# The last FFN step on its own PSUM tiles, its output in halves, and 128-column scores in tile 0

## The chip, the cores and the metric

One core of one Trainium2 chip runs the whole program. The metric is the device time of one execution in microseconds; a smaller number is better. Three executions were timed without the profiler, and one more was profiled.

## The reference

Attention with a window of 96 keys and 8 global keys feeds a feed-forward layer with a rational activation. Everything is fp32; the shapes are batch 4, 8 heads, 768 positions, 64 per head, so 3072 tokens of 512, and 2048 hidden units.

```python
scores = scale * q @ k.T + bias              # kept where key < n_global, or 0 <= rel < n_local
a = softmax(scores)
x = (a @ v).transpose(0, 2, 1, 3).reshape(3072, 512)
h = x @ w_in                                 # 512 x 2048
P = a0 + a1*h + a2*h**2 + a3*h**3
Q = 1 + |b0|*|h| + |b1|*h**2
out = (P / (Q + 1e-6)) @ w_out               # 2048 x 512
```

## The kernel before

The tokens are cut into 24 tiles of 128 queries, six to a batch; two tiles make a chunk of 256 tokens, and there are 12 chunks. Attention goes in 96 units, one for a tile and a pair of heads. A query tile sees its own block of 128 keys and the block before it. Tile 0 of a batch has no block before it: its score product (`st_score`, L407) reads the one block twice by a broadcast, so that it is 256 columns wide like the others, and the softmax reads the first 128 columns alone. That concerns 16 units (4 in each batch), with 4 score products each.

The FFN goes in 96 steps, eight to a chunk, each for 256 hidden units in two halves `y` of 128. A step runs `st_ffn1` (the first product into a PSUM tile `h`, 12 products of 256 columns for each half, since x and w are each split into a high and a low part), `st_ew1` to `st_ew4` (the activation, on ScalarE, VectorE and GpSimd, with `q` in PSUM and `g` in SBUF as its ends) and `st_ffn2` (12 products of 512 columns into the accumulators `acc_0` and `acc_1`, one for each half of the tokens). For chunk 0 the weights are not split yet, and the products are plain fp32 (L249, L328).

The loop over `t` writes the stages down with priorities (the tables `PRI`, `PRI_A`), and a scheduler orders the instructions of each engine when the program is built. During the first 35 steps or so the weights are loaded, decoded and split between the other work (`decode`, `split_w`), for the most part on VectorE.

The last step, 95, is written apart: `is_last(f)` puts its activation through `last_half`, once for each half, with VectorE in GpSimd's place. Both halves lie in one PSUM tile `h95`, and the loop asks for the second half's product behind the first half's activation:

```python
            if is_last(f):
                st_ew4(f - 1)
                last_half(f, 0)
                st_ffn1(f, 1)
                last_half(f, 1)
```

After it the two accumulators are copied out (one on ScalarE, one on VectorE) and SyncE's queue sends each as 128 rows of 2 KB (`st_ffn2`, L339 and L342). Then each engine reads a flag and branches past the general version of the kernel (L671, L672), which these inputs don't need.

Of the kernel before, what the change touches and what calls it, by code (L numbers as in the profile page):

```python
# [9 lines left out]
F32 = mybir.dt.float32  # L10
# [3 lines left out]
AF = mybir.ActivationFunctionType  # L14
# [80 lines left out]
def tile_kernel(ctx: ExitStack, tc: tile.TileContext, q, k, v, n_global, n_local,  # L95
# [144 lines left out]

    def st_ffn1(f, y):
        c, j = divmod(f, FPC)
        if y == 0:
            hps[f] = pl.ps_h.tile(sh, F32, tag="h", name=f"h{f}")
        jw, fw = divmod((2 * j + y) * P, 2 * TOK)
        fs = slice(fw, fw + P)
        if c == 0 and not pl.split:
            for ct in range(NCT):
                nc.tensor.matmul(out=hps[f][:, y, :], lhsT=full[1, ct, jw][:, fs], rhs=xT[c][:, ct, :],  # L249
                                 start=(ct == 0), stop=(ct == NCT - 1))  # L250
            return
        xh, xl = xT[c]
        n = 0
        for ct in range(NCT):
            wh, wl = w_hi((1, ct, jw)), low[1, ct, jw]
            for w, x in ((wh, xh), (wh, xl), (wl, xh)):
                nc.tensor.matmul(out=hps[f][:, y, :], lhsT=w[:, fs], rhs=x[:, ct, :],  # L257
                                 start=(n == 0), stop=(n == 3 * NCT - 1))
                n += 1

# [4 lines left out]
    def is_last(f):  # L265
        return f == NU - 1 and not pl.split
# [4 lines left out]


    def st_ew1(f, ys=BOTH):
        h = hps[f][:, ys]
        if f not in ew:
            ew[f] = {}
        for n in "uas":
            if n not in ew[f]:
                ew[f][n] = tmp(f"f{n}{f}")
        u, a, s = (ew[f][n][:, ys] for n in "uas")  # L280
        nc.scalar.activation(out=u, in_=h, func=AF.Identity, scale=a3, bias=a2)  # L281
        nc.scalar.activation(out=a, in_=h, func=AF.Abs, scale=b0)
        nc.scalar.activation(out=s, in_=h, func=AF.Square, scale=b1)  # L283

    def st_ew2(f, ys=BOTH):
        h = hps[f][:, ys]
        u, a, s = (ew[f][n][:, ys] for n in "uas")
        nc.vector.tensor_tensor(out=u, in0=u, in1=h, op=ALU.mult)  # L288
        nc.vector.scalar_tensor_tensor(out=u, in0=u, scalar=a1, in1=h, op0=ALU.add, op1=ALU.mult)  # L289
        side(f).tensor_tensor(out=a, in0=a, in1=s, op=ALU.add)  # L290


    def st_ew3(f, ys=BOTH):
        if f not in rps:
            rps[f] = pl.ps_r.tile(sh, F32, tag="r", name=f"q{f}")
        a, s = (ew[f][n][:, ys] for n in "as")
        nc.scalar.activation(out=s, in_=a, func=AF.Ln, bias=q1)  # L297
        nc.scalar.activation(out=rps[f][:, ys], in_=s, func=AF.Exp, scale=-1.0)  # L298

    def st_ew4(f, ys=BOTH):  # L300
        u, a, r = ew[f]["u"][:, ys], ew[f]["a"][:, ys], rps[f][:, ys]
        nc.vector.scalar_tensor_tensor(out=u, in0=u, scalar=a0, in1=r, op0=ALU.add, op1=ALU.mult)  # L302
        nc.vector.scalar_tensor_tensor(out=r, in0=a, scalar=q1, in1=r, op0=ALU.add, op1=ALU.mult)  # L303
        nc.vector.scalar_tensor_tensor(out=u, in0=r, scalar=2.0, in1=u, op0=ALU.subtract, op1=ALU.mult,  # L304
                                       reverse0=True)
        if f < FPC and not pl.split:
            gs[f] = u
            return
        if f not in gs:
            gs[f] = pl.ffn.tile([P, 2, 2, TOK], FR, tag="g", name=f"g{f}", bufs=pl.gbufs)  # L310
        g = gs[f]
        nc.scalar.copy(out=g[:, 0, ys], in_=u)  # L312
        side(f).tensor_tensor(out=g[:, 1, ys], in0=u, in1=g[:, 0, ys], op=ALU.subtract)  # L313
# [2 lines left out]
        for st in (st_ew1, st_ew2, st_ew3, st_ew4):  # L316
            st(f, slice(y, y + 1))

    def st_ffn2(f, t):
        c, j = divmod(f, FPC)  # L320
        if j == 0:
            accs[c, t] = pl.ps_o.tile([P, DM], F32, tag="acc", name=f"acc{c}_{t}")
        acc = accs[c, t]
        ts = slice(t * P, (t + 1) * P)
        for y in range(2):
            ft = 2 * j + y
            if c == 0 and not pl.split:
                nc.tensor.matmul(out=acc, lhsT=gs[f][:, y, ts], rhs=full[0, ft],  # L328
                                 start=(ft == 0), stop=(ft == NFT - 1))
                continue  # L330
            wh = w_hi((0, ft))
            for n, (z, w) in enumerate(((0, wh), (0, low[0, ft]), (1, wh))):
                nc.tensor.matmul(out=acc, lhsT=gs[f][:, z, y, ts], rhs=w,  # L333
                                 start=(ft == 0 and n == 0), stop=(ft == NFT - 1 and n == 2))
        if j == FPC - 1:
            o = tmp(f"o{c}_{t}").rearrange("p a b -> p (a b)")
            rows = slice(c * TOK + t * P, c * TOK + (t + 1) * P)
            if is_last(f):
                (nc.vector.tensor_copy if t else nc.scalar.copy)(out=o, in_=acc)  # L339
            else:  # L340
                nc.any.tensor_copy(out=o, in_=acc)
            nc.sync.dma_start(out=out[rows, :], in_=o)  # L342


# [54 lines left out]
    def st_score(u):  # L399
        c, t, p, b, i = unit(u)  # L400
        qT = qTs.pop(u)
        s_ps = pl.ps_t.tile([P, 2, 2, P], F32, tag="t", name=f"s{u}")
        for x in range(2):
            h = 2 * p + x
            rhs = kT[:, h] if i else kT[:, h, 0:1, :].broadcast_to([P, 2, P])
            for z in range(2):
                nc.tensor.matmul(out=s_ps[:, x], lhsT=qT[:, z, x, :], rhs=rhs, start=(z == 0), stop=(z == 1))  # L407
        if 1 <= i < NT - 1:
            nc.gpsimd.tensor_copy(out=kT[:, 2 * p:2 * p + 2, i % 2, 0:G], in_=kG[:, 2 * p:2 * p + 2, :])
        if i == 0:  # L410
            mk = mask0
        else:
            mk = masks[:, 0:2, :] if i % 2 else masks[:, 1:3, :]
        pr = pl.att.tile([P, 2, 2, P], F32, tag="prob", name=f"pr{u}")
        st = stats[:, u % 4]
        for x in range(2):
            h = 2 * p + x
            nc.vector.tensor_tensor_reduce(  # L418
                out=blocks_of(pr[:, x], i), in0=blocks_of(s_ps[:, x], i), in1=mk,
                scale=-(2.0 ** -(h + 1)), scalar=3e38, op0=ALU.add, op1=ALU.min, accum_out=st[:, x:x + 1])  # L420
        prob[u] = (pr, st)
# [71 lines left out]
    def windowed():  # L493
# [17 lines left out]
        for t in range(NU + LAG + F2):  # L511
# [10 lines left out]
            on("score", st_score, t - 2)  # L522
            on("soft", st_soft, t - 2)
            on("ffn1a", st_ffn1, f, 0)
            on("qkT", st_qkT, t)
            if t % 2:
                on("pv", lambda u: st_pv(u // 2), t - 5)
# [8 lines left out]
            if is_last(f):  # L536
                st_ew4(f - 1)
                last_half(f, 0)
                st_ffn1(f, 1)
                last_half(f, 1)  # L540
            else:
                on("ffn1b", st_ffn1, f, 1)
                on("ew1", st_ew1, f)
                if not is_last(f - 1):
                    on("ew4", st_ew4, f - 1)
                on("ew2", st_ew2, f)
            on("ffn2a", st_ffn2, f - F2, 0)
            on("pT", st_pT, t - 3)
            on("ffn2b", st_ffn2, f - F2, 1)
# [161 lines left out]
```

## Time and profile before

| | |
|---|---|
| median of the three timed executions | 796.09 us (795.2 to 796.21) |
| the profiled execution's own time | 793.47 us |
| its span, first to last instruction | 791.7 us |
| TensorE busy, share of the span | 745.0 us, 94% |
| VectorE busy, share of the span | 589.6 us, 74% |
| mean granted clock of TensorE | 0.996 of full speed |

The span is what the trace covers; 1.8 us of the execution's own time lie outside it. A share over the whole span mixes three stages: the start with the weights, the long middle, and the last microseconds.

### The profile page before, as it was taken

To read this page: it belongs to the slowest core of one execution; us is meant where nothing else is said; L and a number is where in the kernel's file an instruction comes from. 1 tells how busy PE (TensorE), PEld (TensorE's weight loads), DVE (VectorE), ACT (ScalarE), POOL (GpSimd) and SP (SyncE) were. 2 spreads that over 40 slices of the span, in tenths; PEclk is the share of its full clock that TensorE was granted. 3 is DMA by queue.
4 is the path that set the end of the run, shared out by engine and by line. 5 is a ranking of instruction groups with operands and counts; after the bars stand their busy time and mean duration, and the time that the engine had idled before them with its cause. 6 is when DMAs were issued, how large, how long until landed. Compare 5 with 4: busy or idle time off the path is not lost.

```text
span 791.7 us, 15480 instructions
## 1 busy us (share of the span) xinstructions
PE 745.0 (94%) x5184; PEld 647.2 (82%) x5184; DVE 589.6 (74%) x1453; ACT 573.0 (72%) x1407; POOL 531.7 (67%) x572
## 2 busy tenths in 40 slices
PE   3678998899999999999999999999999999999995
PEld 2466656598988998988998988988998988988993
DVE  5899998988786767776776767776776767776664
ACT  4688767776786777777777777777777777776763
POOL 3887657998966676675676676675677676664440
PEclk9999999999999999999999999999999999999999
DMA  7884555122121222222222222222222222100000
GB/s 182 233 228 144 158 156 159 44 65 64 43 58 23 62 55 49 62 54 58 57 47 49 61 55 48 61 55 53 63 48 48 61 56 48 41 15 1 27 1 32
DMA packets 101400, 55.90 MB, mean 71 GB/s; under 512 B 81856, under 2 KB 94144, under 8 KB 101312
## 3 DMA queue, kind: packets, MB, share of 16 engines
q1 hardware_dynamic: 101312, 54.82, 26.3%
q8 instruction: 44, 0.72, 0.4%
q14 instruction: 44, 0.36, 0.1%
HBM read 35.92 MB, written 6.29 MB: 53 GB/s over the span
## 4 chain that ended last, share of the span: by engine, by line
PE 81%; DVE 9%; POOL 3%; DMA 2%; issue 2%; ACT 1%; SPq 0%; DVEq 0%; POOLq 0%; ACTq 0%
PE h L257 32%; PE acc L333 30%; PE s L407 5%; PE o L467 5%; PE tp L450 4%; PE tk L377 3%; POOL pr L440 2%; PE acc L328 1%; DMA qT<-qT 1%; DVE pr L418 1%; DMA r<-in_moe_w_out_dram 1%; DVE fu L304 1%; POOL sp L369 1%; DVE fu L288 1%; DVE r L189 1%
## 5 line engine op out<-in xcount | busy, mean ns | idle before, releaser
L333 PE MATMUL acc<-wout_h,g 128*128 128x512 f32 x704 | 250.1, 406 | 0.8 <-ACT g L312 0.8
L257 PE MATMUL h<-xh,win_h 128*128 128x256 f32 x704 | 204.7, 291 | 2.4 <-DVE fu L289 2.4
L440 POOL TENSOR_SCALAR pr<-pr,stats 128x256 f32<-128x256 f32 (+1 forms) x192 | 180.5, 950 | 32.9 <-DVE stats L433 15.5
L257 PE MATMUL h<-xl,win_h 128*128 128x256 f32 x704 | 197.7, 281 | 0.0
L290 POOL TENSOR_TENSOR fa<-fa,fs 128x512 f32<-128x512 f32 x95 | 124.5, 1311 | 91.1 <-ACT fs L283 87.3
L333 PEld LDWEIGHTS acc<-wout_h,g 128*128 128x128 f32 x704 | 128.5, 188 | 23.3 <-ACT g L312 1.2
L257 PEld LDWEIGHTS h<-xh,win_h 128*128 128x128 f32 x704 | 132.5, 188 | 11.3 <-issue 6.6
L369 POOL TENSOR_TENSOR sp<-nat,sp 128x256 fp32r<-128x256 f32 x96 | 75.9, 791 | 95.8 <-DVE sp L368 45.8
L257 PEld LDWEIGHTS h<-xl,win_h 128*128 128x128 f32 x704 | 132.4, 188 | 1.8 <-issue 0.5
L428 ACT ACTIVATE pr<-pr,stats 128x256 f32<-128x256 f32 (+1 forms) x192 | 92.6, 485 | 55.2 <-DVE stats L418 55.0
L281 ACT ACTIVATE fu<-h,coef 128x512 f32<-128x512 f32 (+1 forms) x97 | 75.0, 774 | 60.3 <-PE h L257 59.4
L313 POOL TENSOR_TENSOR g<-fu,g 128x512 fp32r<-128x512 f32 x87 | 112.7, 1295 | 7.9 <-DVE fu L289 4.5
L302 DVE SCALAR_TENSOR_TENSOR fu<-fu,coef,q 128x512 f32<-128x512 f32 (+1 forms) x97 | 71.6, 738 | 48.2 <-ACT q L298 47.2
L297 ACT ACTIVATE fs<-fa,coef 128x512 f32<-128x512 f32 (+1 forms) x97 | 69.6, 718 | 34.9 <-POOL fa L290 32.5
L452 DVE COPY pT<-tp 128x512 f32<-128x512 f32 (+1 forms) x75 | 48.5, 646 | 61.8 <-PE tp L450 61.2
L288 DVE TENSOR_TENSOR fu<-fu,h 128x512 f32<-128x512 f32 (+1 forms) x97 | 65.3, 673 | 12.3 <-ACT fs L283 10.7
L407 PE MATMUL s<-kT,qT 128*128 128x256 f32 x384 | 70.2, 304 | 4.4 <-DMA qT<-qT 3.4
L289 DVE SCALAR_TENSOR_TENSOR fu<-fu,coef,h 128x512 f32<-128x512 f32 (+1 forms) x97 | 71.8, 740 | 2.6
L450 PE MATMUL tp<-ident,pr 128*128 128x128 f32 x352 | 63.0, 282 | 10.7 <-POOL pr L440 10.2
L303 DVE SCALAR_TENSOR_TENSOR q<-fa,coef,q 128x512 f32<-128x512 f32 (+1 forms) x97 | 72.1, 743 | 0.0
L407 PEld LDWEIGHTS s<-kT,qT 128*128 128x128 f32 x384 | 60.4, 199 | 11.6 <-issue 2.4
L283 ACT ACTIVATE fs<-h,coef 128x512 f32<-128x512 f32 (+1 forms) x97 | 66.5, 685 | 0.1
(271 smaller groups left out, 1622.5 us busy)
## 6 DMA issues: line engine op xcount, KB each, us to landing
qT<-qT SPq DMA_DIRECT2D x192, 64.0 KB, 2.1
r<-in_moe_w_in_dram SPq DMA_DIRECT2D x16, 512.0 KB, 5.4
r<-in_moe_w_out_dram SPq DMA_DIRECT2D x16, 512.0 KB, 3.5
nat<-in_q_dram SPq DMA_DIRECT2D x48, 128.0 KB, 2.7
nat<-in_k_dram SPq DMA_DIRECT2D x48, 128.0 KB, 2.5
vt<-in_v_dram SPq DMA_DIRECT2D x48, 128.0 KB, 2.3
out_dram<-o SPq DMA_DIRECT2D x24, 256.0 KB, 2.1
vt<-in_v_dram SPq DMA_DIRECT2D x32, 8.0 KB
```

What stands on the lines that cost most here:

```text
L257: nc.tensor.matmul(out=hps[f][:, y, :], lhsT=w[:, fs], rhs=x[:, ct, :], start=(n == 0), stop=(n == 3 * NCT - 1))
L281: nc.scalar.activation(out=u, in_=h, func=AF.Identity, scale=a3, bias=a2)
L288: nc.vector.tensor_tensor(out=u, in0=u, in1=h, op=ALU.mult)
L290: side(f).tensor_tensor(out=a, in0=a, in1=s, op=ALU.add)
L303: nc.vector.scalar_tensor_tensor(out=r, in0=a, scalar=q1, in1=r, op0=ALU.add, op1=ALU.mult)
L313: side(f).tensor_tensor(out=g[:, 1, ys], in0=u, in1=g[:, 0, ys], op=ALU.subtract)
L333: nc.tensor.matmul(out=acc, lhsT=gs[f][:, z, y, ts], rhs=w, start=(ft == 0 and n == 0), stop=(ft == NFT - 1 and n == 2))
L369: nc.gpsimd.tensor_tensor(out=s[:, :, :, 1, :], in0=n, in1=s[:, :, :, 0, :], op=ALU.subtract)
L407: nc.tensor.matmul(out=s_ps[:, x], lhsT=qT[:, z, x, :], rhs=rhs, start=(z == 0), stop=(z == 1))
L428: nc.scalar.activation(out=d, in_=d, func=AF.Exp, scale=-1.0, bias=st[:, x:x + 1], accum_out=st[:, 2 + 2 * x:3 + 2 * x])
L440: nc.gpsimd.tensor_scalar(out=d, in0=d, scalar1=st[:, 6 + x:7 + x], scalar2=None, op0=ALU.mult)
L450: nc.tensor.transpose(out=t_ps[:, x, w, :], in_=pr[:, x, w, :], identity=ident)
```

## The change

Four edits, of which the diff shows the core.

- The second half of step 95 gets PSUM tiles of its own, for its product (`h95_1`) and for its `q`, both from the pool `ps_t` that the attention used. Its product is asked for together with the first half's.
- The second product of step 95 is written half by half (`y` outermost), where it was written accumulator by accumulator.
- Each accumulator of the last chunk is copied out in two halves of 256 columns, the first by ScalarE, the second by VectorE, and each half is sent by itself: the first from ScalarE's queue, the second from SyncE's.
- The score products of tile 0 are 128 columns wide, without the broadcast.

```diff
     def st_ffn1(f, y):
         c, j = divmod(f, FPC)
-        if y == 0:
-            hps[f] = pl.ps_h.tile(sh, F32, tag="h", name=f"h{f}")
+        if y == 0 or is_last(f):
+            hps[f, y] = (pl.ps_t if y else pl.ps_h).tile(sh, F32, tag="t" if y else "h", name=f"h{f}_{y}")
+        else:
+            hps[f, 1] = hps[f, 0]
...
-        if f not in rps:
-            rps[f] = pl.ps_r.tile(sh, F32, tag="r", name=f"q{f}")
+        y = ys.start
+        rps[f, y] = (pl.ps_t if y else pl.ps_r).tile(sh, F32, tag="t" if y else "r", name=f"q{f}_{y}")
...
-    def st_ffn2(f, t):
+    def st_ffn2(f, t, ys=(0, 1)):
...
             if is_last(f):
-                (nc.vector.tensor_copy if t else nc.scalar.copy)(out=o, in_=acc)
-            else:
-                nc.any.tensor_copy(out=o, in_=acc)
+
+                for x, (copy, queue) in enumerate(((nc.scalar.copy, nc.scalar), (nc.vector.tensor_copy, nc.sync))):
+                    cs = slice(x * DM // 2, (x + 1) * DM // 2)
+                    copy(out=o[:, cs], in_=acc[:, cs])
+                    queue.dma_start(out=out[rows, cs], in_=o[:, cs])
+                return
+            nc.any.tensor_copy(out=o, in_=acc)
             nc.sync.dma_start(out=out[rows, :], in_=o)
...
-            rhs = kT[:, h] if i else kT[:, h, 0:1, :].broadcast_to([P, 2, P])
             for z in range(2):
-                nc.tensor.matmul(out=s_ps[:, x], lhsT=qT[:, z, x, :], rhs=rhs, start=(z == 0), stop=(z == 1))
+                nc.tensor.matmul(out=blocks_of(s_ps[:, x], i), lhsT=qT[:, z, x, :], rhs=blocks_of(kT[:, h], i), start=(z == 0), stop=(z == 1))
...
             on("ffn1a", st_ffn1, f, 0)
+            if is_last(f):
+                st_ffn1(f, 1)
...
                 last_half(f, 0)
-                st_ffn1(f, 1)
                 last_half(f, 1)
...
+            if is_last(f - F2):
+                for y in range(2):
+                    st_ffn2(f - F2, 0, (y,))
+                    st_ffn2(f - F2, 1, (y,))
+                continue
```

What the scheduler makes of it shows at three places. The first is TensorE around the last step. `h_9737` is the PSUM tile of step 95 (of its first half alone, after the change), `g_9719` the activation of step 93, `acc_0_9503` and `acc_1_9510` the accumulators. Before:

```order
L333 MATMUL acc_0_9503<-wout_h,g_9719 128x512
L333 MATMUL acc_1_9510<-wout_h,g_9719 128x512 x2
L333 MATMUL acc_1_9510<-w_11l,g_9719 128x512
L333 MATMUL acc_1_9510<-wout_h,g_9719 128x512
L257 MATMUL h_9737<-xh_8798,win_h 128x256
L257 MATMUL h_9737<-xl_8799,win_h 128x256
L257 MATMUL h_9737<-xh_8798,w_0_3l 128x256
```

After, where `h_1_9750` is the second half's own tile:

```order
L259 MATMUL h_0_9737<-xh_8798,w_3_3l 128x256
L259 MATMUL h_1_9750<-xh_8798,win_h 128x256
L259 MATMUL h_1_9750<-xl_8799,win_h 128x256
L259 MATMUL h_1_9750<-xh_8798,w_2_3l 128x256
L259 MATMUL h_1_9750<-xh_8798,win_h 128x256
L259 MATMUL h_1_9750<-xl_8799,win_h 128x256
L259 MATMUL h_1_9750<-xh_8798,w_3_3l 128x256
L335 MATMUL acc_0_9503<-wout_h,g_9719 128x512
```

The second half's 12 products moved from behind the 12 of step 93 to ahead of them: six stand as shown, and the other six stand still earlier, one at a time or three together, among the products of the steps 88 to 95 and all ahead of the first half's last three. Behind step 93's twelve, TensorE's next rows are now step 94's twelve, which stood behind the second half.

The second place is VectorE's end, after the change, with what each row waits for (`Activation` is ScalarE, `DVE` VectorE itself):

```order
L306 SCALAR_TENSOR_TENSOR fu_9772<-q_0_9781,fu_9772 128x256 [waits DVE_49]
L306 SCALAR_TENSOR_TENSOR fu_9772<-q_1_9796,fu_9772 128x256 [waits DVE_49]
L315 TENSOR_TENSOR g_9787<-fu_9772,g_9787 128x256 [waits Activation_49] x2
L344 COPY o_0_9837<-acc_0_9503 128x256 [waits Activation_49]
L344 COPY o_1_9845<-acc_1_9510 128x256 [waits Activation_49]
```

Before, VectorE had one copy there, of the whole of `acc_1_9510`, and it waited for TensorE; each half copy now waits for ScalarE's copy of the other half of the same accumulator.

The third place is VectorE near row 160 of its program, in the start, where the first activation (`fu_767`) meets the decoding of the weights (`w_0f`, `w_1f` and their raw tiles `r_`). Before:

```order
L175 SCALAR_TENSOR_TENSOR w_0f<-r_0_679,w_0f 128x512
L431 TENSOR_REDUCE stats<-stats 128x2
L177 SCALAR_TENSOR_TENSOR w_0f<-r_0_679,w_0f 128x512
L433 RECIPROCAL stats<-stats 128x2
L208 CAST wout_h<-w_0f 128x512
L189 SCALAR_TENSOR_TENSOR r_1_687<-r_1_687 128x512
L191 SCALAR_TENSOR_TENSOR w_1f<-w_1f,r_1_687 128x512
L208 CAST wout_h<-w_1f 128x512
L288 TENSOR_TENSOR fu_767<-fu_767,h_742 128x512
```

After:

```order
L177 SCALAR_TENSOR_TENSOR w_3f<-r_3_624,w_3f 128x512
L208 CAST wout_h<-w_3f 128x512
L436 TENSOR_REDUCE stats<-stats 128x2
L438 RECIPROCAL stats<-stats 128x2
L290 TENSOR_TENSOR fu_767<-fu_767,h_0_742 128x512
L172 TENSOR_SCALAR w_0f<-w_0f 128x512
L291 SCALAR_TENSOR_TENSOR fu_767<-fu_767,coef,h_0_742 128x512
L173 TENSOR_SCALAR w_0f<-w_0f 128x512
```

All eight rows of decoding for `w_0f` and `w_1f`, which stood ahead of the first activation, stand behind its first row. Shifts of this kind, of up to some 19 rows on VectorE, run through the start on all engines. From attention's unit 37 on (VectorE's row 550 of 1455) up to the last step, VectorE, ScalarE, GpSimd and SyncE have their rows in the same order in both programs, and so has TensorE but for the second half's early products.

## Rows read from the trace of the kernel before

**Rows 1.** The page: busy time by engine, and TensorE's row of 40 slices.

```profile
PE 745.0 (94%) x5184; PEld 647.2 (82%) x5184; DVE 589.6 (74%) x1453; ACT 573.0 (72%) x1407; POOL 531.7 (67%) x572
...
PE   3678998899999999999999999999999999999995
```

**Rows 2.** Busy time by stretch: start, length, engines, granted clock, DMA share, GB/s.

```profile
12.00:153.00 141.00, 113.57 (x628) 81.38 (x628) 132.53 (x339) 105.83 (x283) 104.64 (x108) 0.99 0.60 170
153.00:774.00 621.00, 620.44 (x4506) 557.60 (x4506) 445.29 (x1073) 459.00 (x1102) 422.38 (x452) 1.00 0.19 48
```

**Rows 3.** Timeline, 771 to 787 us: start, length, instruction, idle before and its releaser.

```profile
771.65 0.27 PE L257 MATMUL h<-xh,w_3l 128*128 128x256 f32 x1
...
776.12 0.62 ACT L312 CAST g<-fu 128x512 fp32r<-128x512 f32 x1
...
776.53 0.39 PE L257 MATMUL h<-xh,win_h 128*128 128x256 f32 x1 [1.79 <-DVE fu L289]
...
776.87 1.29 POOL L313 TENSOR_TENSOR g<-fu,g 128x512 fp32r<-128x512 f32 x1 [4.55 <-DVE fu L289]
...
783.23 0.50 PE L333 MATMUL acc<-wout_h,g 128*128 128x512 f32 x1 [0.79 <-ACT g L312]
...
783.57 0.40 PE L333 MATMUL acc<-w_15l,g 128*128 128x512 f32 x1
...
784.26 0.63 PE L333 MATMUL acc<-wout_h,g 128*128 128x512 f32 x2
784.70 0.58 ACT L339 COPY o<-acc 128x512 f32<-128x512 f32 x1 [1.52 <-PE acc L333]
784.93 0.69 DVE L339 COPY o<-acc 128x512 f32<-128x512 f32 x1 [1.29 <-PE acc L333]
785.31 1.52 SPq L342 DMA_DIRECT2D out_dram<-o  x2
```

**Rows 4.** The chain that ended last: start, length, what.

```profile
152.75 3.70 PE acc L328 x8
...
156.46 2.83 PE h L257 x24
```

**Rows 5.** Groups of 256-column copies from PSUM: count, busy us, mean ns.

```profile
L452 ACT COPY pT<-tp 128x256 f32<-128x256 f32 x4 | 1.5, 370 | 0.5 <-PE tp L450 0.4
L452 DVE COPY pT<-tp 128x256 f32<-128x256 f32 x12 | 5.0, 418 | 9.2 <-PE tp L450 9.2
```

**Rows 6.** The line that sends the output: issue time on the queue, min/median/max ns.

```profile
L342 SPq DMA_DIRECT2D out_dram<-o x24: 332/367/1093, 157.1 to 785.7; - x24
```

**Rows 7.** Timeline around one tile 0 score in the middle.

```profile
555.41 0.64 PE L407 MATMUL s<-kT,qT 128*128 128x256 f32 x4
...
555.89 0.28 PE L257 MATMUL h<-xh,win_h 128*128 128x256 f32 x1
```

**Rows 8.** Timeline around 128-column transposes; PEld is the weight load.

```profile
289.52 0.46 PE L377 MATMUL tk<-ident_r,sp 128*128 128x128 f32 x4
...
289.79 0.19 PEld L257 LDWEIGHTS h<-xh,win_h 128*128 128x128 f32 x1
289.82 0.35 PE L257 MATMUL h<-xh,win_h 128*128 128x256 f32 x1
289.89 0.19 PEld L257 LDWEIGHTS h<-xl,win_h 128*128 128x128 f32 x1
```

**Rows 9.** Weight loads by line: duration ns min/median/max, then first and last start.

```profile
L407 PEld LDWEIGHTS s<-kT,qT x384: 186/188/338, 7.5 to 710.6; 128*128 128x128 f32 x192
...
L377 PEld LDWEIGHTS tk<-ident_r,sp x384: 137/142/224, 5.0 to 697.8; 128*128 128x128 f32 x192
```

**Rows 10.** VectorE's waits from 12 to 153 us: total, times, longest.

```profile
DVE stats L431 <- ACT pr L428: 1.9, 1, 1.9
```

**Rows 11.** Timeline in the start, around the first activation.

```profile
60.35 0.67 ACT L283 ACTIVATE fs<-h,coef 128x512 f32<-128x512 f32 x1
...
62.47 0.68 DVE L288 TENSOR_TENSOR fu<-fu,h 128x512 f32<-128x512 f32 x1
```

More of the change, by code (lines that the diff above doesn't have):

```diff
@@ L248, in st_ffn1 @@
             for ct in range(NCT):
-                nc.tensor.matmul(out=hps[f][:, y, :], lhsT=full[1, ct, jw][:, fs], rhs=xT[c][:, ct, :],
+                nc.tensor.matmul(out=hps[f, y][:, y, :], lhsT=full[1, ct, jw][:, fs], rhs=xT[c][:, ct, :],
                                  start=(ct == 0), stop=(ct == NCT - 1))
@@ L256, in st_ffn1 @@
             for w, x in ((wh, xh), (wh, xl), (wl, xh)):
-                nc.tensor.matmul(out=hps[f][:, y, :], lhsT=w[:, fs], rhs=x[:, ct, :],
+                nc.tensor.matmul(out=hps[f, y][:, y, :], lhsT=w[:, fs], rhs=x[:, ct, :],
                                  start=(n == 0), stop=(n == 3 * NCT - 1))
@@ L273, in st_ew1 @@
     def st_ew1(f, ys=BOTH):
-        h = hps[f][:, ys]
+        h = hps[f, ys.start][:, ys]
         if f not in ew:
@@ L285, in st_ew2 @@
     def st_ew2(f, ys=BOTH):
-        h = hps[f][:, ys]
+        h = hps[f, ys.start][:, ys]
         u, a, s = (ew[f][n][:, ys] for n in "uas")
@@ L293, in st_ew3 @@
     def st_ew3(f, ys=BOTH):
-        if f not in rps:
-            rps[f] = pl.ps_r.tile(sh, F32, tag="r", name=f"q{f}")
+        y = ys.start
+        rps[f, y] = (pl.ps_t if y else pl.ps_r).tile(sh, F32, tag="t" if y else "r", name=f"q{f}_{y}")
         a, s = (ew[f][n][:, ys] for n in "as")
         nc.scalar.activation(out=s, in_=a, func=AF.Ln, bias=q1)
-        nc.scalar.activation(out=rps[f][:, ys], in_=s, func=AF.Exp, scale=-1.0)
+        nc.scalar.activation(out=rps[f, y][:, ys], in_=s, func=AF.Exp, scale=-1.0)
     def st_ew4(f, ys=BOTH):
-        u, a, r = ew[f]["u"][:, ys], ew[f]["a"][:, ys], rps[f][:, ys]
+        u, a, r = ew[f]["u"][:, ys], ew[f]["a"][:, ys], rps[f, ys.start][:, ys]
         nc.vector.scalar_tensor_tensor(out=u, in0=u, scalar=a0, in1=r, op0=ALU.add, op1=ALU.mult)
@@ L317, in last_half @@
             st(f, slice(y, y + 1))
-    def st_ffn2(f, t):
+    def st_ffn2(f, t, ys=(0, 1)):
         c, j = divmod(f, FPC)
-        if j == 0:
+        if j == 0 and 0 in ys:
             accs[c, t] = pl.ps_o.tile([P, DM], F32, tag="acc", name=f"acc{c}_{t}")
@@ L324, in st_ffn2 @@
         ts = slice(t * P, (t + 1) * P)
-        for y in range(2):
+        for y in ys:
             ft = 2 * j + y
@@ L334, in st_ffn2 @@
                                  start=(ft == 0 and n == 0), stop=(ft == NFT - 1 and n == 2))
-        if j == FPC - 1:
+        if j == FPC - 1 and 1 in ys:
             o = tmp(f"o{c}_{t}").rearrange("p a b -> p (a b)")
```

## The prediction

> **What bounds the kernel now.** I read the page first, then busy time by stretch, then the timeline of the last 20 us, and the chain that ended last. The page gives TensorE 94% of the span, and its slices show where the rest is lost: in the first eight, and in the last [rows 1]. By stretch there are three stages. From 12 to 153 us VectorE is busy 132.5 of 141 us and TensorE 113.6: VectorE sets the pace. From 153 to 774 us TensorE is busy 620.4 of 621 us at full clock, so each microsecond of its work there is one of the span [rows 2]. From 774 us on it waits: 1.79 us for VectorE to finish reading `h95`, since the second half's product writes the same PSUM tile, and 0.79 us for the last `g`. Then come the copies, the two sends, and 4.9 us from the end of the second send's issue (785.31 + 1.52 = 786.83) to the span's end at 791.7 [rows 3].
>
> All sums are made against the profiled execution, 793.47 us with 1.8 us outside its span. The median is 796.09, 2.6 us above it; I carry the difference over to the median. A measurement of this kernel tells apart from no change what is over 0.2%, 1.59 us.
>
> **The last step.** A product of 256 columns takes 0.118 us of TensorE (24 in 2.83 us) [rows 4], one of 512 columns 0.234 us start to start, and 0.40 from its start to its end (from 783.57 to 784.26 three have started, 0.23 each, and the last two together take 0.63) [rows 3]. Six of the second half's products now stand ahead of the first half's last three, and TensorE has no gap there, so the first half ends 6 x 0.118 = 0.70 us later: 771.92 becomes 772.62. Behind it ScalarE, VectorE and GpSimd do step 94's activation in the order that they had, up to GpSimd's low part of `g94`, 776.87 + 1.29 = 778.16 before [rows 3], 778.86 now.
>
> Before, that low part was hidden: TensorE did the second half's 12 products from 776.53. Now it has step 93's twelve (2.8 us, to 776.1), waits for the high part of `g94` (776.12 + 0.62, 0.70 later: 777.44), does four products, and waits for the low part. From 778.88 on it has 20 products, eight of step 94 and twelve of step 95. The second half's activation must be ready for them. Behind step 94's last VectorE row (which ends at 776.8 by the same shift) VectorE has twelve operations of 256 columns, at 0.33 to 0.40 us each, of which the first half's `g` needs nine; by my sum it is there at 780.65, TensorE asks at 780.75, and each later piece is 0.5 us or more early. So the last product starts at 778.88 + 19 x 0.234 = 783.32 and ends 0.40 later at 783.72. Before it was 784.26 + 0.63 = 784.89. **Gain 1.17 us.** Bounds: 1.87 if the six early products cost nothing, because gaps that the records hide take them; 0.7 if the slack of 0.1 turns into a wait of 0.5. That the second product is written in two parts costs and brings nothing by itself: the scheduler already had the halves in that order.
>
> **The copies and sends.** The accumulators end at 783.49 and 783.72. A copy of 256 columns from PSUM takes 370 ns on ScalarE and 418 ns on VectorE [rows 5]. The halves of one accumulator don't go side by side: VectorE's copy waits for ScalarE's. ScalarE: 783.53 to 783.90, then 783.85 to 784.22. VectorE: 783.93 to 784.35, then to 784.68. Before, two whole copies lay side by side and ended at 785.28 and 785.62, the second 0.73 us behind the last product [rows 3]; now it is 0.96 us. SyncE's second send is issued 0.1 us later, at 784.79. Its issue took 1.09 us before, the longest of the line's 24, whose median is 0.37 [rows 6]; nothing in the profile says why. If the long issue comes again, SyncE is done at 785.88, 2.16 us behind the last product against 1.94 before, a **loss of 0.22**; if not, a gain of 0.5. I take the long issue, since its nearest row is the same instruction in the same place. The transfers themselves are hidden: 4.9 us lie behind the last issue, and half a row is half the bytes. ScalarE now issues two sends ahead of its branch; at 0.37 to 1.09 us each it is done by 785.9 too, so I give it nothing, with 0.5 as the upper bound.
>
> On this the Trainium skill speaks against the edit: "PSUM — Partial Sum Buffer", section "PSUM bank collisions raise a hardware error", says that ScalarE and VectorE must not use one bank at the same time, reads against reads included, and that software has to keep them apart. Only the wait in VectorE's order bears that out so far; the rows show whole copies side by side in two banks. By the rule the term is the 0.22 us above; without it VectorE's second copy would end at 784.17 and the term would be a gain of 0.3.
>
> **The narrower scores.** 16 units have four each, 64 products. The first 16 lie in the start, where TensorE has gaps; 48 lie in the dense stretch. Four take 0.48 us now (555.41 to 555.89) [rows 7]. How long a 128-column product of this kind takes no row shows, so I bound it. The columns alone: transposes of 128 columns go four in 0.30 us (289.52 to 289.82) [rows 8], 0.075 each. But their weight load takes 142 ns and that of a score 188 ns [rows 9]. Rows 8 show what such a load costs behind a narrow product: the load for the next product starts at 289.79, the one behind that only at 289.89, some 0.10 us on, and the product between them takes 0.35 us where its like take 0.28. Its last 0.28 us begin at 289.89, so the load held it back for 0.10 to 0.11 us. I take the load as the pace, 0.11 us for 0.12 now: 48 x 0.01, **gain 0.5 us**. Ends: a gain of 48 x 0.045 = 2.2 us at the transposes' pace; a loss, should narrow products of this kind run at the pace of plain fp32, whose 512 columns take two records of 0.46 us (eight in 3.70 us) [rows 4], so 0.23 us for 128: 48 x 0.11 = 5.3 us.
>
> **The start.** The scheduler laid the start out anew. The work is the same and VectorE sets the pace, so only its idle time can change: 141 less 132.5 us by stretch, in waits of up to 1.9 us [rows 2, 10]. I take 0, with 3 us either way: less than half of those 8.5 us won, or as much again added.
>
> **Sum.** -1.17 + 0.22 - 0.5 + 0 = -1.45 us: 792.0 by the profiled execution's own time, 794.6 by the median.
>
> **Rivals.**
> - The new order stalls VectorE, and the kernel gets slower. Eight rows of decoding that covered the first activation's inputs now stand behind it. ScalarE finished that input at 60.35 + 0.67 = 61.02, VectorE used it at 62.47, 1.45 us later [rows 11]. Eight rows of about 0.65 us are 5.2 us less cover; if ScalarE is no earlier, VectorE stands 3.7 us. For it: VectorE can't pass a waiting row by, and everything behind waits. Against: ScalarE's rows moved forward too. It decides from 3.0 us on (1.45 and 1.59); at 3.7 the time is 798.3.
> - The new order removes waits of [rows 10], some 3 us: 791.6. For it: the activation of chunk 0 comes earlier on all engines, so TensorE gets its plain fp32 products earlier. Against: VectorE's sum of work to the last activation of chunk 0 is the same.
> - The narrow scores run at the pace of their columns, 2.2 us in place of 0.5: 792.9. The Trainium skill's "TensorE: Matmul & The Clock Gate", section "Wait — 56ns, not 53.3ns?", gives N / 2.4 GHz plus 2.5 ns from start to start, 56 ns for 128 columns; by that estimate the gain would be 48 x 0.064 = 3.1 us. No run here shows it. Against it stands the load of 188 ns.
> - The narrow scores run at plain fp32's pace, 5.3 us: 794.6 + 0.5 + 5.3 = 800.4. For it: the kernel's only narrow products of this type are transposes, which prove little for a score. Against: no row at all.
> - The halved output brings nothing or costs, which I already count; without the long issue (0.72 us less) 793.9.
>
> **Chances and range.** The forecast as summed, with the start within 1.5 us: 0.42, 793.1 to 796.1, of which 0.17 is faster by over 0.2% and 0.25 within it. The start costs: 0.20 (0.12 slower, 0.08 within). The start wins: 0.15 (0.14 faster). Scores at column pace: 0.10, faster. Scores at plain fp32's pace: 0.13 (0.11 slower). That makes 0.41 faster, 0.36 the same, 0.23 slower. The predicted time is 794.6. The range from 791.2 to 799.2 holds the two start cases and column pace, and leaves out the slow scores and the far ends, less than 2 in 10.
>
> **What would show it.** In the profile after: no wait of TensorE for L291 (the old L289) near 774 us, and one for GpSimd's low part of `g94`; from there 20 products 0.234 us apart; ScalarE's copies ahead of VectorE's, and a last issue of SyncE near 1.09 us. Scores of tile 0 four in 0.44 us in the dense stretch: 0.30 or 0.9 would be the rivals. TensorE dense from 153 us on, within 1.5 us; another time there, with longer waits of VectorE ahead of it, is a start case. I am wrong outright if the start moves by more than 3 us or the last step's activation, not GpSimd, turns out to be what TensorE waits for.

## The result, and the profile after

The changed kernel takes 799.62 us (median of 6 executions, 796.20 to 801.47) beside 795.52 us for the kernel before (6, 793.87 to 796.21) on the same chip: a ratio of 1.0055, 95% interval 1.0038 to 1.0073. It is 4.1 us slower, where 1.45 us faster was forecast. The profiled execution took 801.37 us with a span of 799.6, one of the longer ones, so its differences to the span of before (791.7) add up to 7.9 us.

The page after, busy time by engine and TensorE's 40 slices, against [rows 1]:

```profile
PE 749.5 (94%) x5184; PEld 654.1 (82%) x5184; DVE 591.0 (74%) x1454; ACT 573.6 (72%) x1408; POOL 526.9 (66%) x572
...
PE   2789797999989999999999999999999999999995
```

Busy time by stretch after, the two stretches of [rows 2] (columns as there):

```profile
12.00:153.00 141.00, 114.00 (x577) 83.97 (x577) 125.19 (x326) 102.58 (x274) 95.69 (x104) 0.94 0.59 167
153.00:774.00 621.00, 616.29 (x4512) 554.62 (x4511) 449.76 (x1079) 456.62 (x1099) 422.39 (x453) 1.00 0.19 48
```

Two things are to be seen. By 153 us VectorE has done 7.3 us less work (125.19 against 132.53), and the granted clock is 0.94 where it was 0.99. And the stretch that was dense has holes: 616.29 of 621 us. Of the 4.7 us, 1.4 are one wait ahead of 163 us, where the start hasn't ended yet; the largest behind it is a wait that the kernel before doesn't have. TensorE and VectorE in the changed kernel, from 225 us on (timeline):

```profile
225.26 1.19 DVE L374 CAST sp<-nat 128x256 fp32r<-128x256 f32 x1
226.37 0.68 DVE L457 COPY pT<-tp 128x512 f32<-128x512 f32 x1
226.97 0.67 DVE L290 TENSOR_TENSOR fu<-fu,h 128x512 f32<-128x512 f32 x1
227.56 0.41 DVE L423 CUSTOM_DVE_ANT_0 pr<-s,masks 128x256 f32<-128x256 f32 x1
...
228.85 0.73 DVE L291 SCALAR_TENSOR_TENSOR fu<-fu,coef,h 128x512 f32<-128x512 f32 x1
229.64 0.39 PE L259 MATMUL h<-xh,win_h 128*128 128x256 f32 x1 [2.39 <-DVE fu L291]
```

L291 is the last row that reads one `h` tile, and TensorE's next FFN step writes into that tile. A cast, a copy, two score rows and L306 stand ahead of it on VectorE. In the start, VectorE's waits (12 to 153 us; total, times, longest), against [rows 10]:

```profile
DVE pr L423 <- PE tp L455: 3.0, 2, 2.6
DVE w_1f L172 <- ACT w_1f L170: 2.6, 2, 1.7
DVE fu L290 <- ACT fs L285: 2.4, 2, 1.6
```

The first activation of [rows 11], on VectorE, comes behind such a wait, though no later than before (62.09 us, 62.47 before):

```profile
62.09 0.69 DVE L290 TENSOR_TENSOR fu<-fu,h 128x512 f32<-128x512 f32 x1 [1.64 <-ACT fs L285]
```

The tail, against [rows 3] (timeline; the sends are one group for each queue):

```profile
785.17 0.62 ACT L314 CAST g<-fu 128x512 fp32r<-128x512 f32 x1
785.84 0.50 PE L335 MATMUL acc<-wout_h,g 128*128 128x512 f32 x1 [1.36 <-ACT g L314]
785.92 1.29 POOL L315 TENSOR_TENSOR g<-fu,g 128x512 fp32r<-128x512 f32 x1 [4.70 <-DVE fa L292]
787.26 0.73 PE L335 MATMUL acc<-wout_h,g 128*128 128x512 f32 x2 [0.23 <-POOL g L315]
791.54 0.62 PE L335 MATMUL acc<-wout_h,g 128*128 128x512 f32 x2
791.96 0.65 ACT L344 COPY o<-acc 128x256 f32<-128x256 f32 x2 [2.70 <-PE acc L335]
792.36 0.76 DVE L344 COPY o<-acc 128x256 f32<-128x256 f32 x2 [2.65 <-ACT o L344]
792.36 0.86 ACTq L345 DMA_DIRECT2D out_dram<-o  x2
792.82 0.83 SPq L345 DMA_DIRECT2D out_dram<-o  x2
```

TensorE no longer waits for L291 there. It waits for the two parts of `g94`, and VectorE's half copies start when ScalarE's end. The tile 0 scores of [rows 7], and the product behind them (timeline):

```profile
563.81 0.56 PE L412 MATMUL s<-kT,qT 128*128 128x128 f32 x4
564.20 0.33 PE L259 MATMUL h<-xh,win_h 128*128 128x256 f32 x1
564.37 0.28 PE L259 MATMUL h<-xl,win_h 128*128 128x256 f32 x1
```

Four take 0.39 us, not 0.48, but the product behind them now holds TensorE 0.17 us instead of 0.12.

### The profile page after: what moved, and what is told of

Its sections match the earlier page's. It is cut to its first block, busy times and chain, and to the rows that moved or that the text cites. A ratio compares the mean times of both kernels' runs of the same rounds, so it can differ in the third digit from the quotient of the medians.

```text
span 799.6 us, 15467 instructions
## 1 busy us (share of the span) xinstructions
PE 749.5 (94%) x5184; PEld 654.1 (82%) x5184; DVE 591.0 (74%) x1454; ACT 573.6 (72%) x1408; POOL 526.9 (66%) x572
## 4 chain that ended last, share of the span: by engine, by line
## 5 line engine op out<-in xcount | busy, mean ns | idle before, releaser
L445 POOL TENSOR_SCALAR pr<-pr,stats 128x256 f32<-128x256 f32 (+1 forms) x192 | 175.6, 925 | 34.8 <-DVE stats L438 28.7
L375 POOL TENSOR_TENSOR sp<-nat,sp 128x256 fp32r<-128x256 f32 x96 | 74.3, 774 | 100.8 <-DVE sp L374 52.2
L290 DVE TENSOR_TENSOR fu<-fu,h 128x512 f32<-128x512 f32 (+1 forms) x97 | 65.4, 674 | 14.2 <-ACT fs L285 12.6
L291 DVE SCALAR_TENSOR_TENSOR fu<-fu,coef,h 128x512 f32<-128x512 f32 (+1 forms) x97 | 71.7, 740 | 2.6
L412 PE MATMUL s<-kT,qT 128*128 128x256 f32 (+1 forms) x384 | 69.3, 303 | 4.0 <-DMA qT<-qT 4.0
L455 PE MATMUL tp<-ident,pr 128*128 128x128 f32 x352 | 64.8, 287 | 7.8 <-POOL pr L445 7.0
L412 PEld LDWEIGHTS s<-kT,qT 128*128 128x128 f32 x384 | 61.2, 203 | 11.4 <-DMA qT<-qT 4.3
```

The lines of the kernel that those rows point to most:

```text
L375: nc.gpsimd.tensor_tensor(out=s[:, :, :, 1, :], in0=n, in1=s[:, :, :, 0, :], op=ALU.subtract)
L412: nc.tensor.matmul(out=blocks_of(s_ps[:, x], i), lhsT=qT[:, z, x, :], rhs=blocks_of(kT[:, h], i), start=(z == 0), stop=(z == 1))
L445: nc.gpsimd.tensor_scalar(out=d, in0=d, scalar1=st[:, 6 + x:7 + x], scalar2=None, op0=ALU.mult)
```

## The experiments

Four theories stood at first: S, that the new order of the start costs (my rival with VectorE's stall); W, that the narrow products cost; and that the last step's edits, or the halved copies, do. Ratios are against the kernel before on the same chip, with 95% intervals. Two starts of products from each trace serve as marks: the last plain fp32 product of chunk 0, which ends the start, and the FFN product that stands at 298.90 us before. What lies between them is the dense stretch's own.

### One edit at a time

**e1_narrow_only**, the kernel before with the narrow scores alone:

```diff
-            rhs = kT[:, h] if i else kT[:, h, 0:1, :].broadcast_to([P, 2, P])
-                nc.tensor.matmul(out=s_ps[:, x], lhsT=qT[:, z, x, :], rhs=rhs, ...)
+                nc.tensor.matmul(out=blocks_of(s_ps[:, x], i), lhsT=qT[:, z, x, :], rhs=blocks_of(kT[:, h], i), ...)
```

> The kernel before with the narrow scores of tile 0 alone. Its start has the instruction order of the changed kernel, its last step that of the kernel before. Theory S (the new order of the start costs the time): about 4.1 us of the measured difference plus the 1 us or so that the last step gives back, so 4 to 6 us slower than before, and TensorE reaches the FFN product that stood at 303 us some 6 to 9 us later. Rival W (the narrow products themselves, or the last step and its copies, cost it): within 1 us of before, TensorE at most 1 us later at 303 us.

Measured: 801.98 us, ratio 1.0076 (1.0049 to 1.0103); TensorE stands 8.7 us later at the second mark of its trace. The whole loss comes with this one edit.

**e2_own_tile**, the changed kernel's last step without its copies and without the narrow scores:

```diff
-        if y == 0:
-            hps[f] = pl.ps_h.tile(sh, F32, tag="h", name=f"h{f}")
+        if y == 0 or is_last(f):
+            hps[f, y] = (pl.ps_t if y else pl.ps_h).tile(...)
...
+            if is_last(f - F2):
+                for y in range(2):
+                    st_ffn2(f - F2, 0, (y,))
+                    st_ffn2(f - F2, 1, (y,))
```

> The kernel before with the last step's own PSUM tiles and the last second product in two parts alone: wide scores, whole output copies as before. Its start has the order of the kernel before. By the prediction's sum of the last step: last product 1.17 us earlier, span 1.2 us shorter; by the changed kernel's profile, in which the last product stood 7.3 us later while the steps ahead of it stood 8.3 us later, 1.0 us. Rival (the last step is what costs): 1 us or more slower than before.

Measured: 793.24 us, ratio 0.9992 (0.9978 to 1.0006). It costs nothing; whether it wins the time of one execution cannot tell.

**e3_halves_out**, the copies and sends in halves alone:

```diff
-                (nc.vector.tensor_copy if t else nc.scalar.copy)(out=o, in_=acc)
+                for x, (copy, queue) in enumerate(((nc.scalar.copy, nc.scalar), (nc.vector.tensor_copy, nc.sync))):
+                    cs = slice(x * DM // 2, (x + 1) * DM // 2)
+                    copy(out=o[:, cs], in_=acc[:, cs])
+                    queue.dma_start(out=out[rows, cs], in_=o[:, cs])
```

> The kernel before with the output copies and sends of the last chunk in halves alone; everything ahead of them in the order of before. By the prediction's sum: 0.22 us slower with the long issue of SyncE's second send, 0.5 us faster without it. By the changed kernel's profile, whose span ended 0.6 us later than its last product alone would have it: 0.6 us slower. Rival (it is the bulk of the slowdown): 3 us or more slower.

Measured: 793.86 us, ratio 0.9991 (0.9981 to 1.0002): not the loss. In its profile two issues, one on each queue, took 2.5 and 2.1 us.

**e4_narrow_late**, the changed kernel with `wide = u < 48`: narrow scores in the eight last tile 0 units only. The scheduler then leaves the order of before as it was, but for the last step.

> The changed kernel with wide scores in units 0 to 3 and 24 to 27, narrow ones in the eight tile-0 units from 48 on alone, so that the start has the order of the kernel before. Theory S: the slowdown is gone, TensorE stands where it stood before at 303 us within 1 us, and gains 0.08 us at each of the eight units (0.7 us by 600 us); with the last step's 1.0 gained and the copies' 0.6 lost 1.1 us faster than before. Rival W (narrow products, last step or copies cost): still 2 us or more slower.

Measured: 792.82 us, ratio 0.9980 (0.9971 to 0.9989). The slowdown is gone, and this version beats both kernels.

### The order without the edit, the edit without the order

Issue-order edges between neighbours on each engine pin the first 190 to 240 us to an order that was read from the other kernel; no other instruction changes. The table holds some 2,600 instruction numbers.

```diff
+def pin(tc, nc):
+    made = {i.name: i for i in nc.cur_bb.bb.instructions}
+    dep = mybir.DependencyInfo(mybir.DependencyClass.NoSync, mybir.DependencyReason.DATA)
...
+        for a, b in zip(row, row[1:]):
+            tc.add_manual_dep(made[f"I-{b}"], f"I-{a}", dep, reason="start order")
```

**e5_narrow_old_order** and **e6_wide_new_order**:

> Narrow scores in all tile-0 units, and the last step of before, with every engine's order of the first 190 us or so pinned to that of the kernel before by issue-order edges. It has the very instructions of e1_narrow_only in the order of before. Theory S (the order costs, not the products): the loss is gone, and twelve units at 0.08 to 0.09 us each are won in the dense stretch: about 1 us faster than before. Rival W (the narrow products in the start cost, by letting TensorE idle longer and fall to its lower clock): 3 us or more slower, as e1_narrow_only.

> The kernel before, wide scores and all, with its order pinned to the changed kernel's up to 240 us or so. Theory S: the loss is there without one narrow product: 5 to 8 us slower than before. Rival W: within 1 us of before.

Measured: e5 793.79 us, ratio 0.9989 (0.9978 to 1.0001); e6 800.94 us, ratio 1.0069 (1.0049 to 1.0088). With not one narrow product, the changed order costs 5.5 us; with all narrow products, the old order costs nothing. W has fallen. Busy time by stretch, first e5, then e6:

```profile
12.00:160.00 148.00, 119.55 (x666) 86.76 (x666) 138.64 (x353) 111.06 (x294) 111.06 (x113) 0.99 0.58 166
...
220.00:240.00 20.00, 20.00 (x145) 18.02 (x145) 15.63 (x36) 16.44 (x39) 13.62 (x15) 1.00 0.21 60
```

```profile
12.00:160.00 148.00, 121.52 (x628) 89.42 (x628) 133.98 (x343) 107.24 (x284) 100.18 (x108) 0.90 0.57 162
...
220.00:240.00 20.00, 17.61 (x129) 15.64 (x129) 14.88 (x34) 15.71 (x35) 13.60 (x16) 1.00 0.22 60
```

The narrow scores' own gain was expected too high in e5 (1 us). Between the marks at 298.90 and 511.16 us lie four of the units: 212.26 us before, 212.09 in e5, so 0.04 us each: 0.09 less in the four products, 0.05 more in the one behind them. The four units behind 511 us win as much (273.73 us from there to the last product's end in before, 273.55 in e9). The four ahead of 298.90 win nothing that shows (143.04 us between the marks below in before, 143.09 in e5). That makes about 0.35 us for the twelve.

**e7_old_start_new_rest** and **e8_new_start_old_rest** join the two orders at one seam:

> As e1_narrow_only, but the order is that of before up to 157 us and the changed kernel's behind it. The changed kernel's TensorE has a wait of 2.4 us near 228 us, for the activation's second VectorE row (L291), that before doesn't have. Theory S2 (the order behind the start costs by itself): that wait is there, and the run is 1.5 to 3 us slower than before. Rival S1 (the start alone costs, the wait is its consequence): no such wait, and 1 us faster than before.

> As e1_narrow_only, but the order is the changed kernel's up to 161 us and that of before behind it; the output copies of the chunks but the last are put on ScalarE by hand, where before has them. Theory S1 (the order of the start costs): 4 to 6 us slower than before, TensorE's last plain fp32 product of chunk 0 at 160 to 162 us where it was 156, and no wait near 228 us. Rival S2 (the order behind it is what costs): within 1 us of before.

Measured: e7 803.27 us, ratio 1.0108 (1.0088 to 1.0128); e8 798.68 us, ratio 1.0051 (1.0034 to 1.0069). Both parts cost. TensorE's waits in e7 (timeline; line 371 is L257, 403 is L289 in this file):

```profile
168.68 0.50 PE L447 MATMUL acc<-wout_h,g 128*128 128x512 f32 x1 [1.25 <-ACT g L426]
...
229.21 0.38 PE L371 MATMUL h<-xh,win_h 128*128 128x256 f32 x1 [2.38 <-DVE fu L403]
```

The wait near 228 us is there behind the old start as well. The seam made waits of its own (1.25 us here, 3.16 near 173, and 1.26 near 171 in e8), so the two ratios are too high as prices of the parts. The marks of the traces are cleaner (us; e9 to e14 are described below):

```
                          end of start   second mark   between
before                       155.86        298.90       143.04
e5, e4, e14 (old order)  156.12 155.41 156.57           143.09 143.10 143.07
e2, e3, e13 (old order)  159.77 156.94 159.58           142.99 143.12 143.00
changed                      162.29        307.57       145.28
e1, e6 (new order)       160.87 161.38                  146.73 145.30
e9, e11 (new order)      162.14 159.46                  146.51 145.20
e8 (new start, old rest)     159.30        303.78       144.48
e10, e12 (two rows)      158.06 158.80                  142.98 142.93
```

Between the marks the new order costs 2.2 us in the changed kernel, e6 and e11, and 3.5 to 3.7 in e1 and e9. All five have the wait of 2.4 us near 228 us. Behind it the granted clock stays at full in the first three, as in e6's last line above, and falls for a while in the other two. Busy time by stretch in e1:

```profile
220.00:240.00 20.00, 17.61 (x121) 15.86 (x120) 14.25 (x30) 14.98 (x34) 12.68 (x14) 0.91 0.22 60
```

The end of the start differs by 4 us between traces of one order. In e2 and e13 the clock fell at 155.2 us. Measured against before, the last plain products there come 1.7 us later than the rows just ahead of them do; both profiles are of executions some 4 us above their medians.

### Single rows put back in the new order

**e9_one_decode_row**, **e10_two_rows_228**, **e11_cover_activation** and **e12_all_three** are e1_narrow_only, pinned to its own order, with one, two, four and seven rows moved. VectorE's order in e9 and e10, and in the last line what e11 moves, as a difference to e1 (lines of its file):

```diff
 L175 w1_1_2f
+L177 w1_1_2f
 L486 xl, L288 fu3, L302 fu2, L303 q2, L172 w0_6f
-L177 w1_1_2f
...
+L288 fu, L289 fu
 L368 sp, L451 pT
-L288 fu
 L417 pr (twice), L304 fu of the step before
-L289 fu
...
+ScalarE: L170 w0_0f, ahead of L281 fu0; VectorE: L172, L173, L175 w0_0f, ahead of L288 fu0
```

> The kernel of e1_narrow_only with its order pinned, and one VectorE row moved: the last decoding row of the input weights w1_1_2f stands ahead of five rows that it stood behind (xl, three of the activation, one of w0_6f). TensorE waits 3.1 us for it near 91 us and then runs at its lower clock for 6 us. Theory A (that wait and the clock behind it cost): TensorE's wait falls to 1 us or less, its granted clock stays at full there, and the last plain fp32 product of chunk 0 comes 2 to 4 us earlier than in e1_narrow_only. Rival V (VectorE is busy in that stretch and sets the pace, so that the wait lies beside it): the wait goes, but the last product of chunk 0 moves by less than 0.7 us.

Measured: 802.76 us, ratio 1.0099 (1.0081 to 1.0118). TensorE and the clock near 91 us, from 85 us on in e1 and then in e9 (busy time by stretch):

```profile
85.00:91.00 6.00, 3.11 (x15) 1.75 (x13) 6.00 (x10) 3.67 (x11) 2.70 (x3) 1.00 0.46 136
91.00:98.00 7.00, 6.81 (x24) 5.71 (x25) 7.00 (x21) 4.16 (x9) 2.58 (x3) 0.76 0.46 124
```

```profile
85.00:92.00 7.00, 7.00 (x31) 4.95 (x29) 6.97 (x13) 3.65 (x11) 2.52 (x3) 0.96 0.48 125
92.00:100.00 8.00, 8.00 (x33) 5.33 (x32) 8.00 (x20) 5.66 (x11) 5.19 (x5) 1.00 0.34 98
```

The wait is gone and the granted clock is all but full (0.96, then 1.00: 2.4 GHz), where behind the wait it was 0.76 in e1, and 0.53 in the changed kernel (92 to 99 us), close to the 1.2 GHz level. Nothing is won: the time isn't below e1's, and the last plain product of chunk 0 stands at 162.14 us, 160.87 in e1. VectorE is busy all through, as V has it. TensorE's wait of 3.1 us and its slow products lay beside the path.

> The kernel of e1_narrow_only with its order pinned, and two VectorE rows moved: the activation's two rows that read one FFN tile (L288, L289) stand ahead of the four pieces of work (cast, copy, two score rows) that stood ahead of or between them. Theory S2: TensorE's wait of 2.4 us near 228 us is gone, TensorE stands 2.4 us earlier at 300 us, and the run is 2.4 us faster than e1_narrow_only, that is 3 to 5 us slower than before. Rival (the work that was put back becomes late instead): another wait of 1 us or more by 300 us, and less than 1 us won.

Measured: 798.22 us, ratio 1.0040 (1.0027 to 1.0054), by the ratios 2.9 us under e1, which ran on another chip. VectorE's rows and TensorE in e10 (timeline; 402 and 403 are L288 and L289, 371 is L257):

```profile
221.04 0.68 DVE L402 TENSOR_TENSOR fu<-fu,h 128x512 f32<-128x512 f32 x1
221.76 0.75 DVE L403 SCALAR_TENSOR_TENSOR fu<-fu,coef,h 128x512 f32<-128x512 f32 x1
222.42 0.29 DVE L482 CAST sp<-nat 128x256 fp32r<-128x256 f32 x1
...
222.88 0.28 PE L371 MATMUL h<-xh,win_h 128*128 128x256 f32 x1
```

L403 ends 0.37 us before TensorE asks, and nothing becomes late instead: between the marks it takes 142.98 us, as before. That is 3.75 us less than in e1, the wait and the slow clock behind it, and 2.3 less than in the changed kernel, the wait alone.

> The kernel of e1_narrow_only with its order pinned, and the first activation covered again: ScalarE's decoding row of w0_0f stands ahead of the first activation's rows, and three VectorE rows of the same decoding ahead of the activation's first. My rival on record put 3.7 us on that place; the changed order's profiles show 1.65 us of waiting there. Theory C (that wait is passed on to the end of the start): VectorE's wait near 60 us is gone, the last plain fp32 product of chunk 0 comes 1.3 to 1.7 us earlier, 1.5 us faster than e1_narrow_only. Rival V (later waits take it back): less than 0.7 us.

Measured: 800.28 us, ratio 1.0084 (1.0062 to 1.0105). VectorE now waits 1.32 us for ScalarE's decoding row at 59.63 in place of 1.66 for the activation: 0.3 us net. So another wait took the place of the first, and by its ratio the kernel is no faster than e1 (1.0084 against 1.0076). By that the rival V holds.

> The three edits of e9_one_decode_row, e10_two_rows_228 and e11_cover_activation together: seven rows moved, the rest in the changed kernel's order. Theory (these three places are the loss): 5 to 7 us faster than e1_narrow_only, within 1.5 us of before. Rival (the loss is spread over many small waits of the new order): 2.5 to 4 us faster than e1_narrow_only, still 3 us or more slower than before.

Measured: 798.22 us, ratio 1.0044 (1.0030 to 1.0057), the same as e10 alone: the rival holds. What is left is 3.4 us. Nothing of it lies between the marks. Some 0.5 us lie in the last step: with the two rows moved, the scheduler set seven rows of the last step in another order too, and from the product at 511.16 us (before) to the last product's end e12 takes 274.06 us, e11 273.54. The rest lies in the start; that it is spread there over many waits, as the rival has it, isn't shown.

### The rest, and the version without the order

**e13_changed_old_order** is the changed kernel pinned to the old order, **e14_whole_copies** the same with whole copies and SyncE's two sends. **e15_new_to_80** and **e16_new_80_to_161** cut the start's order at 80 us.

> The changed kernel, all four edits, with its order of the first 190 us or so pinned to that of the kernel before: the change without the new order. Theory S: 1.0 us won by narrow scores, 0.9 by the last step, 0.2 to 0.7 lost by the copies: 1.2 to 1.7 us faster than before. Rival (the edits together cost something that no single edit showed): no faster than before.

> As e13_changed_old_order, but with whole output copies and SyncE's two sends as before. By the profiles (6.5 to 6.8 us from the last product's end to the span's end with whole copies, 7.4 with halves): 0.6 us faster than e13_changed_old_order, 1.9 us faster than before. Rival (the halves cost nothing outside a profile; the kernel with halves alone timed 0.1% under before): within 0.3 us of e13_changed_old_order.

Measured: e13 792.69 us, ratio 0.9980 (0.9965 to 0.9994); e14 793.30 us, ratio 0.9981 (0.9967 to 0.9996). The four edits without the new order win 1.6 us, and with e6's 5.5 us that gives 3.9 of the 4.1 measured. Whole and halved copies can't be told apart by time; by the profiles the last product's end lies 7.43 us ahead of the span's end with halves and 6.53 with whole copies.

> As e1_narrow_only, but the changed kernel's order stands only up to 80 us and that of before behind it. VectorE's waits over 0.3 us come to 5.7 us by 80 us in the new order and 3.5 in the old. Theory (the first part of the start's order costs): the last plain fp32 product of chunk 0 at 158 to 160 us, 2 to 3 us slower than before. Rival (the second part costs): 156 to 157 us, and no slower than before.

> As e1_narrow_only, but the changed kernel's order stands only between 80 and 161 us, with that of before ahead of it and behind it. Theory (the first part costs, this one little): the last plain fp32 product of chunk 0 at 156 to 157.5 us, within 1.2 us of before. Rival (the second part costs, by VectorE's waits near 120 to 133 us): 158 to 160 us, 2 to 3 us slower than before.

Measured: e15 801.16 us, ratio 1.0082 (1.0068 to 1.0097); e16 799.66 us, ratio 1.0062 (1.0049 to 1.0074). Both are inconclusive: the seam makes VectorE wait 4.06 us in e15 and 2.77 in e16, near 89 us, as much as what was to be split or more.

## Why the prediction was wrong

**The step that failed** is "The start. [...] I take 0, with 3 us either way", and with it what the paragraph left out: the scheduler's new order did not end at 153 us. It reaches to 250 us or so (VectorE's row 550, as the section on the change has it), into the stretch of which the prediction itself says that each microsecond of TensorE's work is one of the span. There no row was priced, and there lies one wait of 2.39 us that two moved rows remove (e10), and that costs 3.7 us where the clock falls behind it (e1). In the start the new order costs about 3 us more: the start ends at 158.1 to 162.3 us in eight traces of the new order (changed, e1, e6, e8 to e12; mean 160.3), at 155.4 to 159.8 in eight of the old (before, e2 to e5, e7, e13, e14; mean 157.1). The two ranges overlap, so the 3 us are a difference of means. VectorE's waits over 0.3 us from 12 to 160 us come to 9.8 to 14.7 us in the eight new ones (mean 11.4), 5.6 to 8.3 in the eight old ones (mean 7.0). That fits the argument that only VectorE's idle time can change; that it would not change much was a guess. Most of what is added lies ahead of 80 us: 6.2 to 10.3 us of these waits there in the new order, 3.0 to 4.3 in the old; behind 80 us it is 1.7 to 4.5 and 2.5 to 4.0. Which rows make it stays open. Two places of the start were put back in e12 without a gain there, and cutting the order adds waits at the cut.

**The rival that came closest** (the new order stalls VectorE, 798.3) had the sign and nearly the size, the size by luck. That VectorE waits longer in the new start is right. The place it named has a wait too, L290 for the first activation, but of 1.64 us, not 3.7, with the row no later than before, and in e11 covering it brings 0.3. Of the rest, the wait near 228 us was in no rival. The start's costing had 0.20 of the chance.

**Without the new order** the forecast of 1.45 us looks good beside the 1.6 of e13. By the profiles the terms add up to less: 1.0 us won by the last step and 0.35 by the scores, 0.6 to 0.9 lost by the copies, so 0.45 to 0.75 won. The interval of e13 reaches from 0.5 to 2.8 us, so its time neither confirms the terms nor contradicts them. What the new last step may win by meeting a slow clock less often (below) had no term in the forecast.

**The last step**: 1.17 us forecast. From one FFN product at 511 us (before) to the last product's end, kernels with narrow scores and the old last step take 273.54 and 273.55 us (e11, e9), those with the new one 272.51 to 272.54 (changed, e4, e13, e14): 1.0 us. These are the traces in which the clock stayed at full there. It fell behind TensorE's wait in 8 of the 13 traces with the old last step (last section), and in one of the five with the new one (e2: 274.26 us, with wide scores). By the prediction's sum TensorE idles 1.2 us for the high part of `g94` and 0.3 for the low part; it is 1.36 and 0.23, and then 20 products take 0.237 us each. As forecast, it waits for these two parts and not for the last step's own activation.

**The copies**: the second copy ends 0.96 us behind the last product, as forecast. SyncE's long issue did not come (issues of 332 and 403 ns; in e3 two long ones did), but the span still ends 0.6 to 0.9 us later than with whole copies, where 0.22 was the sum: 5.9 us from the last issue's end, not the 4.9 of [rows 3]. With whole copies and no long issue it is 5.3 (e5, e14). What the last microseconds wait for isn't settled. ScalarE's and VectorE's copies of one accumulator take turns in the tail's rows above, as the order of the program has it. The Trainium skill, "PSUM — Partial Sum Buffer", section "PSUM bank collisions raise a hardware error", asks for that; no run here lets both engines read one bank at once.

**The narrow scores**: 0.5 us forecast, about 0.35 measured, and at the pace of the weight load: three of the four products take 0.11 us to the next start, as forecast. The product behind them takes 0.17 us instead of 0.12; its own load, 0.19 us, begins only at 564.14 and is still running when it starts at 564.20, where before it began 0.11 us ahead of its product (555.78 and 555.89). The rivals at column pace and at plain fp32's pace are out. The Trainium skill's 56 ns for 128 columns ("TensorE: Matmul & The Clock Gate", section "Wait — 56ns, not 53.3ns?") is near what the first of each four shows, 58 to 60 ns to the next start.

## What to carry to other kernels

A change that makes one instruction cheaper for the scheduler is two changes: pin the old order and time each alone before either is credited with the result. In reading a new order, look first, in the stretch where the bottleneck is dense, at the rows that free a tile it needs next: two rows, some 1.4 us of work moved behind other work, cost more here than all four edits brought. A wait of TensorE is no price by itself: in the start, a 3.1 us wait and the half clock behind it cost nothing that shows, while VectorE set the pace; near 228 us a 2.4 us wait cost all of itself.

## What the runs showed of the hardware

In the last step TensorE waits 1.8 us for VectorE before its second half, in all kernels with the old last step. In some executions the granted clock stays at full behind it, in others it falls to the 1.2 GHz level for some three microseconds, with the same instructions ahead. Busy time by stretch of e1, from the wait on:

```profile
784.00:786.00 2.00, 1.14 (x6) 1.14 (x7) 1.41 (x4) 1.33 (x3) 0.79 (x1) 0.76 0.00 0
786.00:788.00 2.00, 2.00 (x10) 1.90 (x10) 0.70 (x2) 0.29 (x1) 0.49 (x1) 0.50 0.02 4
788.00:790.00 2.00, 2.00 (x9) 1.60 (x8) 0.97 (x3) 1.41 (x5) 0.00 (x0) 0.89 0.02 4
```

From step 95's first product to the last product's end e1 took 17.50 us, the kernel before 16.40, where the clock did not fall: 1.1 us by chance, as much as the last step's edit is worth. Of the 13 traces with the old last step it fell in 8, which took 16.9 to 17.5 us, and stayed at full in 5, which took 16.4 us (e12, with its other order of the last step, 16.9). The executions of the new order also differ more among themselves (796.0 to 803.3 us in e1) than those of before beside them (792.9 to 796.4).
